# Three pairs of a second MLP product taken by quarters, seven products for eight, in the last passage of a transformer block

## The chip, the core and the metric

The kernel runs on one core of a Trainium2 chip. Five engines work side by side, each through its own list of instructions in order: TensorE (PE) multiplies, VectorE (DVE), ScalarE (ACT) and GpSimd (POOL) work on tiles of 128 partitions, and SyncE (SP) issues most of the transfers. They wait for one another through semaphores. The metric is the device time of one execution in microseconds (us).

## What is computed

```
x = A_x                                            # 2048 rows of 512, float32
h = x + attention(layernorm(x) @ wqkv) @ wo        # 32 heads, window of 8 at distance 2
r = relu(layernorm(h) @ w1 + b1)                   # 512 -> 1792
out = h + (r * r) @ w2 + b2                        # 1792 -> 512
```

## The kernel before

All matrices are split in a high and a low part of a shorter float format, and a product is the sum of three: high by high, high by low, low by high. `hi` (L152, on ScalarE) makes the high part, `lo` (L155, on VectorE or GpSimd) the low one. The 2048 rows are worked in four passages (`u` = 0 to 3) of four tiles of 128 rows. The 1792 columns of `w1` are 14 blocks `f` of 128.

In passages 0 to 2 the first product of a block is 12 matmuls of 512 columns (L231) and the second product 12 more (`mlp2`, L924), into four accumulators in PSUM, one for each row tile. These passages also hold the attention and are the same in both kernels, in instructions and in order.

The change lies in the last passage (`u` = 3), L1212 to L1271. There the blocks go in seven pairs (`PAIRS`). The **first** product of a pair is already taken by quarters with seven products for eight (Strassen's scheme in Winograd's form): `products_a` has four of the seven (24 matmuls of 256 columns, L837) and `products_b` three (18). For it the weights `w1` are loaded raw (`t_load`), combined (`t_sums`, four subtractions of 256 columns a pair, on GpSimd from the third pair) and split (`t_split`). The results are put together by additions on VectorE (L855, L867, L868, L870: each reads PSUM) and one on GpSimd (L869, `r<-u,p`), then biased, rectified and squared on ScalarE (L866, L873, L879, L884) and split (`squared`). The **second** product, `mlp2`, still takes 12 matmuls of 512 columns a block, 24 a pair. One such block follows `products_a` and one `products_b` of a later pair, and the last ones close the kernel, one row tile after the other; each finished tile is added to `h` (L932, L949) and stored. The rows `h` were given the second bias (`add_b2`, L694, on GpSimd) and put away in DRAM (`spill`) in passage 2, and come back by `unspill` in this one.

The order within an engine is written out by hand: `at(k, f, ...)` puts a call `k` slots ahead, `end_slot` runs the calls of a slot, and an engine's list is the order in which the calls are made. A `row` tile is one of 15 buffers in turn; who asks for one waits until its last user is done.

## Time and profile before

| | |
|---|---|
| median of 3 runs (lowest to highest) | 500.95 us (500.95 to 501.98) |
| the profiled execution | 500.91 us, of which the span from the first to the last instruction is 499.1 us |
| granted TensorE clock | 1.000 |
| PE busy | 494.2 us, 99% of the span, 2411 matmuls |
| PE weight load busy | 420.6 us, 84% |
| DVE, ACT, POOL busy | 383.7 (77%), 305.7 (61%), 354.6 us (71%) |
| chain that ended last | PE 98%, DMA 1% |

To read it: the chain of waits is followed back from the last instruction, at each step to what released it. Here it is TensorE nearly throughout, so that engine waits for nothing and what the others do is hidden. The shares are means over the whole kernel; the change touches the last 75 us alone, where TensorE is busy throughout and the other engines have idle stretches.

### The profile page before, as it was taken

How to read it: one execution, taken by the hardware profiler on the slowest of the kernel's cores; microseconds unless marked ns; L12 is line 12 of the kernel's file. 1: busy time of each engine (PE TensorE's matmuls, PEld its weight loads, DVE VectorE, ACT ScalarE, POOL GpSimd, SP SyncE). 2: the span in 40 equal slices, each digit the busy share in tenths (PEclk: the TensorE clock that was granted, in tenths of full speed). 3: DMA queues.
4: the chain of work that ended last, by engine and by line, in shares of the span. 5: the costliest groups of instructions: out<-in, count | busy, mean ns of one | idle time of the engine just before them, and what ended most of it. 6: DMA issues, size and time to landing. Idle time of an engine off the chain costs nothing.

```text
span 499.1 us, 7514 instructions
## 1 busy us (share of the span) xinstructions
PE 494.2 (99%) x2411; PEld 420.6 (84%) x2411; DVE 383.7 (77%) x526; ACT 305.7 (61%) x543; POOL 354.6 (71%) x429
## 2 busy tenths in 40 slices
PE   8999999999999999999999999999999999999997
PEld 7998888888888888888888888888888888998986
DVE  6479899999989989998979989897984257733233
ACT  4634778668346757478564556866454968766551
POOL 5714798996775999888878777787889353885610
PEclk9999999999999999999999999999999999999999
DMA  8779979889788899689776945977680575355212
GB/s 269 201 215 244 281 253 297 272 268 310 209 219 260 294 286 259 185 226 248 219 253 210 218 143 164 269 236 258 201 202 14 130 193 163 117 158 169 64 42 87
DMA packets 113584, 103.67 MB, mean 208 GB/s; under 512 B 33672, under 2 KB 82056, under 8 KB 113544
## 3 DMA queue, kind: packets, MB, share of 16 engines
q1 hardware_dynamic: 112600, 102.66, 70.1%
q10 hardware_dynamic: 944, 0.52, 0.3%
q8 instruction: 19, 0.31, 0.3%
q14 instruction: 21, 0.17, 0.1%
HBM read 72.65 MB, written 24.25 MB: 194 GB/s over the span
## 4 chain that ended last, share of the span: by engine, by line
PE 98%; DMA 1%; ACT 0%; ACTq 0%; DVE 0%; issue 0%
PE mm L231 49%; PE acc L924 30%; PE wo L231 9%; PE mm L837 7%; PE tr L204 2%; DMA wraw<-in_A_wqkv_dram 1%; PE half L947 0%; ACTq L570 0%; ACT big_h L152 0%; ACT xh L152 0%; DVE h L949 0%
## 5 line engine op out<-in xcount | busy, mean ns | idle before, releaser
L414 POOL TENSOR_TENSOR pr<-pr 128x512 f32<-128x512 f32 (+1 forms) x128 | 134.1, 1048 | 35.6 <-DVE pr L357 30.2
L231 PE MATMUL mm<-big_l,w_h 128*128 128x512 f32 x336 | 88.5, 390 | 0.0
L357 DVE TENSOR_TENSOR pr<-ex,v 128x1024 f32<-128x1024 f32 x62 | 75.6, 1221 | 12.0 <-POOL o L414 9.2
L344 DVE TENSOR_TENSOR pr<-qp,k 128x1024 f32<-128x1024 f32 x64 | 76.8, 1200 | 6.1 <-ACT qp L271 3.3
L380 DVE TENSOR_REDUCE ex<-pr 128x64 f32<-128x1024 f32 x64 | 78.4, 1225 | 1.8
L231 PEld LDWEIGHTS mm<-big_l,w_h 128*128 128x128 f32 x336 | 63.0, 188 | 13.4 <-ACT r L894 0.3
L155 POOL TENSOR_TENSOR rl<-r,rh 128x512 fp32r<-128x512 f32 x42 | 54.9, 1306 | 24.2 <-ACT rh L152 20.1
L231 PE MATMUL mm<-big_l,xh 128*128 128x512 f32 (+1 forms) x208 | 56.3, 379 | 0.0
L231 PE MATMUL mm<-big_h,xh 128*128 128x512 f32 (+1 forms) x208 | 53.1, 377 | 0.3 <-ACT xh L152 0.3
L231 PE MATMUL mm<-big_h,xl 128*128 128x512 f32 (+1 forms) x208 | 52.6, 374 | 0.0
L924 PE MATMUL acc<-big_h,rh 128*128 128x512 f32 x190 | 52.1, 391 | 0.0
L924 PE MATMUL acc<-big_l,rh 128*128 128x512 f32 x190 | 52.0, 390 | 0.0
L924 PE MATMUL acc<-big_h,rl 128*128 128x512 f32 x190 | 51.7, 390 | 0.0
L231 PE MATMUL mm<-big_l,w_l 128*128 128x512 f32 x168 | 44.9, 389 | 0.0
L231 PEld LDWEIGHTS mm<-big_h,xl 128*128 128x128 f32 x208 | 38.3, 188 | 6.0
L231 PEld LDWEIGHTS mm<-big_h,xh 128*128 128x128 f32 x208 | 37.9, 188 | 6.1 <-ACT xh L152 0.5
L924 PEld LDWEIGHTS acc<-big_h,rl 128*128 128x128 f32 x190 | 35.7, 188 | 7.4
L924 PEld LDWEIGHTS acc<-big_l,rh 128*128 128x128 f32 x190 | 35.6, 188 | 7.4
L231 PEld LDWEIGHTS mm<-big_l,xh 128*128 128x128 f32 x208 | 37.4, 188 | 4.9
L924 PEld LDWEIGHTS acc<-big_h,rh 128*128 128x128 f32 x190 | 35.1, 188 | 7.1 <-DVE h L932 0.3
L894 ACT ACTIVATE r<-mm,b_sb 128x512 f32<-128x512 f32 x42 | 28.7, 684 | 16.2 <-PE mm L231 15.7
L231 PEld LDWEIGHTS mm<-big_l,w_l 128*128 128x128 f32 x168 | 31.5, 188 | 6.6
(167 smaller groups left out, 919.4 us busy)
## 6 DMA issues: line engine op xcount, KB each, us to landing
k<-qkv_d SPq DMA_DIRECT2D x50, 288.0 KB, 3.2
v<-qkv_d SPq DMA_DIRECT2D x46, 288.0 KB, 3.2
qkv_d<-y SPq DMA_DIRECT2D x18, 512.0 KB, 4.0
big_l<-w2l_d SPq DMA_DIRECT2D x24, 256.0 KB, 3.1
xt<-in_A_x_dram SPq DMA_DIRECT2D x16, 256.0 KB, 4.2
q<-qkv_d SPq DMA_DIRECT2D x32, 128.0 KB, 3.6
h<-in_A_x_dram SPq DMA_DIRECT2D x16, 256.0 KB, 3.3
h_d<-h SPq DMA_DIRECT2D x16, 256.0 KB, 3.4
```

The lines of the kernel that those rows point to most:

```text
L155: eng.tensor_tensor(out=dst, in0=src, in1=h, op=ALU.subtract)
L204: nc.tensor.transpose(tr[:, k, :], src[:, k * P:(k + 1) * P], ident)
L231: nc.tensor.matmul(ps, l(k), r(k), start=(n == 0), stop=(n == 3 * KB - 1))
L344: nc.vector.tensor_tensor(out=pr.rearrange("p i w h d -> p i w (h d)"), in0=qps["now"][:, j % 2].unsqueeze(2).to_broadcast([P, RI, W, GC]) ...
L357: nc.vector.tensor_tensor(out=p2, in1=vwin, op=ALU.mult, in0=e1[:, :, :, j * GH:(j + 1) * GH].unsqueeze(4).to_broadcast([P, RI, W, GH, DH]))
L380: nc.vector.tensor_reduce(out=lf[:, :, :, j * GH:(j + 1) * GH], in_=pr, axis=X, op=ALU.add)
L414: nc.gpsimd.tensor_tensor(out=dst, in0=p2[:, :, :w], in1=p2[:, :, w:2 * w], op=ALU.add)
L837: nc.tensor.matmul(ps, sta[y][:, k], mov[x][:, k], start=(first and q == 0), stop=(last and q == len(terms) - 1), skip_group_check=True)
L894: nc.scalar.activation(r, ps, AF.Relu, bias=b1_sb[:, f:f + 1])
L924: nc.tensor.matmul(acc[j], l[:, j * P:(j + 1) * P], w[f], start=(first and n < len(js)), stop=(last and n >= len(terms) - len(js)))
```

## The change

The second products of the first four pairs stay as they are. Those of the last three pairs, (0, 7), (1, 8) and (4, 11), are taken by quarters, with seven products of 256 columns: 42 matmuls a pair in place of 24 of 512. `part` makes one of the seven. For this:

- the two blocks of `w2` of each of these pairs are loaded raw again (`v_load`, six transfers of 256 KB), combined on GpSimd (`v_sums`, four subtractions of 256 columns a pair) and split (`v_split`: two `hi` on ScalarE, two `lo` of 512 columns on GpSimd);
- the squared activations of each of these pairs, kept whole, are combined on VectorE (`s_sums`, four operations of 256 columns on two tiles in SBUF) and split (`s_split`, two `hi` on ScalarE, two `lo` on VectorE). The parts lie in columns of `w1_h` and `w1_l` that are no longer needed, as do now all split activations of this passage (`parted`), half of the first block's alone;
- seven products are summed over the three pairs in PSUM (`outer`, `inner`) and put together at the end: one copy on ScalarE, four additions of 512 columns on VectorE, and eight additions of 256 columns into `h` (two on VectorE, six on GpSimd);
- of the whole second products one now follows `products_a` of each pair, none `products_b`, and two are left after the last pair;
- the preparation of `w1` for the first products is moved ahead by one to two pairs, its raw tiles go to other buffers, and `th` is made in two halves;
- tiles 14 and 15 get the second bias after they have come back, by GpSimd, between the two last `v_split`;
- `last_tile` goes, and the last tile is finished in two halves as before, by other products.

```diff
@@ -50,6 +50,10 @@
 HL = (13, 0), (13, 1), (15, 0), (15, 1)
 ENDS = [2, 9, 3, 10]
 PAIRS = (2, 9), (3, 10), (5, 12), (6, 13), (0, 7), (1, 8), (4, 11)
+WN = 3
+PLAN = {n: (1, 0) for n in range(1, 7)}
+VS = {2: 0, 3: 1, 4: 2}
+VP = ()
...
@@ -707,6 +711,8 @@
             lambda k: wo_h[:, k, :], lambda k: wo_l[:, k, :], lows_last=t in OV)
         for n, (fn, a) in zip(slots, ((h_add, (t, ps)), (h_norm, (t,)), (add_b2, (t,)),
                                       (spill, (t,)))):
+            if fn is add_b2 and t >= 14:
+                continue
             (at if fn is h_add or fn is h_norm and t >= 14
...
     def t_split(n):
-        h, l = t_tile(n, "th", F32R), t_tile(n, "tl", F32R)
-        hi(h, tw[n])
-        for k, eng in ((2, nc.vector if n < 3 else nc.gpsimd), (0, nc.gpsimd)):
-            lo(eng, l[:, k:k + 2], tw[n][:, k:k + 2], h[:, k:k + 2])
+        h, l = t_tile("th", "pr"), t_tile("tl", "o")
+        raw = tw[n]
+        for k in (1, 0):
+            hi(h[:, 2 * k:2 * k + 2], raw[k])
+        for k, eng in ((1, nc.vector), (0, nc.gpsimd)):
+            lo(eng, l[:, 2 * k:2 * k + 2], raw[k], h[:, 2 * k:2 * k + 2])
         tw[n] = h, l
...
     def squared(f, r):
-        rh, rl = work.tile([P, D], F32R, name="rh", bufs=LAG + 1), row("rl", dt=F32R)
         nc.scalar.activation(r, r, AF.Square)
-        hi(rh, r)
-        lo(nc.vector, rl, r, rh)
-        hid[R - 1, f] = rh, rl
+        if f in PAIRS[-1]:
+            at(0, parted, f, r)
+        else:
+            parted(f, r)
+    def parted(f, r):
+        rh, rl = [w[:, :, f * P:(f + 1) * P] for w in (w1_h, w1_l)]
+        n = RI if f in WINO[:WN] else R
+        src = r.rearrange("p (j c) -> p j c", j=R)[:, :n]
+        hi(rh[:, :n], src)
+        lo(nc.vector, rl[:, :n], src, rh[:, :n])
+        hid[R - 1, f] = [lambda j, a=a: a[:, j] for a in (rh, rl)]
...
+    PLAIN = len(PAIRS) - WN
+    WINO = [p[i] for i in range(2) for p in PAIRS[PLAIN:]]
+    whole, vw = {}, {}
+    def v_load(q):
+        vw[q] = row("vraw"), row("vraw")
+        for r, f in zip(vw[q], PAIRS[PLAIN + q]):
+            nc.sync.dma_start(r, w2[f * P:(f + 1) * P, :])
+    def v_sums(q):
+        (b11, b12), (b21, b22) = [(r[:, :HD], r[:, HD:]) for r in vw[q]]
+        tt, sub = (nc.vector if q in VP else nc.gpsimd).tensor_tensor, ALU.subtract
+        tt(out=b11, in0=b12, in1=b11, op=sub)
+        tt(out=b12, in0=b22, in1=b12, op=sub)
+        tt(out=b22, in0=b22, in1=b11, op=sub)
+        tt(out=b21, in0=b21, in1=b22, op=sub)
+    def v_split(q):
+        if q == 0:
+            t = [work.tile([P, D], F32R, name="rh", bufs=LAG + 1) for _ in range(4)]
+        else:
+            t = [a[:, i] for a in [att.tile([P, 2, D], F32R, name="vs", tag=tag, bufs=3)
+                                   for tag in ("pr", "o")] for i in range(2)]
+        raw = vw[q]
+        vw[q] = t[:2], t[2:]
+        for i in range(2):
+            hi(t[i], raw[i])
+            at(int(q < 2), lo, nc.gpsimd, t[2 + i], raw[i], t[i])
+    def s_sums(n):
+        rf, rg = whole.pop(n)
+        (a11, a21), (a12, a22) = [(r[:, :HD], r[:, HD:]) for r in (rf, rg)]
+        x = whole[n] = row("x"), row("x")
+        tt, sub = nc.vector.tensor_tensor, ALU.subtract
+        tt(out=x[0][:, :HD], in0=a21, in1=a22, op=ALU.add)
+        tt(out=x[1][:, :HD], in0=a11, in1=a21, op=sub)
+        tt(out=x[0][:, HD:], in0=x[0][:, :HD], in1=a11, op=sub)
+        tt(out=x[1][:, HD:], in0=a12, in1=x[0][:, HD:], op=sub)
+    def s_split(n):
+        for x, f in zip(whole.pop(n), PAIRS[n - PLAIN]):
+            src = x.rearrange("p (j c) -> p j c", j=R)
+            h, l = [w[:, :, f * P:(f + 1) * P] for w in (w1_h, w1_l)]
+            hi(h, src)
+            lo(nc.vector, l, src, h)
+    def part(n, m, ps, js, first=False, last=False):
+        q, (f, g) = n - PLAIN, PAIRS[n]
+        c, d = PAIRS[q]
+        col, i0 = {1: (f, 0), 2: (g, 0), 4: (g, 2), 5: (c, 0), 6: (c, 2), 7: (d, 0), 3: (d, 2)}[m]
+        sta = [w[:, :, col * P:(col + 1) * P] for w in (w1_h, w1_l)]
+        lo_, hi_ = slice(0, HD), slice(HD, D)
+        if m < 4:
+            w, cs = f if m == 1 else g, hi_ if m == 3 else lo_
+            mov = w2_h[w][:, cs], w2_l[w][:, cs]
+        else:
+            i, cs = {5: (0, lo_), 7: (0, hi_), 4: (1, lo_), 6: (1, hi_)}[m]
+            mov = [t[i][:, cs] for t in vw[q]]
+        terms = [(x, y, j) for x, y in ((0, 0), (1, 0), (0, 1)) for j in js]
+        for k, (x, y, j) in enumerate(terms):
+            nc.tensor.matmul(ps[j], sta[x][:, i0 + j], mov[y], start=first and k == 0,
+                             stop=last and k >= len(terms) - len(js), skip_group_check=True)
...
-    fs = [f for pair_ in PAIRS for f in pair_]
-    need = [f for f in fs if f < 12 and f not in place]
+    fs = [f for pair_ in PAIRS[:PLAIN] for f in pair_]
+    need = [f for f in fs + WINO if f < 12 and f not in place]
...
+    AHEAD = {"0a": ((t_split, 1),), "0b": ((t_load, 3), (t_sums, 2)),
+             "1a": ((t_split, 2), (t_sums, 3)), "1b": ((t_load, 4), (t_split, 3), (t_sums, 4)),
+             "2b": ((t_load, 5), (t_split, 4), (t_sums, 5)),
+             "3b": ((t_load, 6), (t_split, 5), (t_sums, 6)), "4b": ((v_sums, 0), (t_split, 6), (v_sums, 1)), "5b": ((v_sums, 2),)}
...
     for n in range(len(PAIRS)):
-        if n + 2 < len(PAIRS):
-            t_load(n + 2)
+        if n in VS:
+            v_load(VS[n])
         products_a(n)
         if not n:
-            at(0, t_split, 1)
+            ahead("0a")
             lo(nc.vector, a_l[4], s32[4], a_h[4])
         if n:
+            if n == len(PAIRS) - 1:
+                at(0, s_sums, n - 2)
             at(0, second, n - 1)
-            if n + 1 < len(PAIRS):
-                at(0, t_split, n + 1)
-            second_product()
-        if n in (4, 5):
-            for i in range(2):
-                at(0, unspill, R * u + 2 * (n - 4) + i)
+            ahead(f"{n}a")
+            if n - 3 in VS and not VS[n - 3]:
+                at(0, v_split, 0)
+            if n == len(PAIRS) - 1:
+                at(0, s_split, n - 2)
+                at(0, v_split, 1)
+            for _ in range(PLAN[n][0]):
+                second_product()
         end_slot(5.6)
         products_b(n)
-        if n + 2 < len(PAIRS):
-            at(0, t_sums, n + 2)
-        if n > 1:
+        ahead(f"{n}b")
+        for _ in range(PLAN[n][1] if n else 0):
             second_product()
         if n == len(PAIRS) - 1:
             at(0, second, n)
-            second_product(True)
+            at(0, s_sums, n - 1)
+            at(0, s_sums, n)
+            at(0, s_split, n - 1)
+            at(0, at, 0, s_split, n)
+            for i in (2, 3, 0, 1):
+                at(1, unspill, R * u + i)
+            for i in (2, 3):
+                at(1, add_b2, R * u + i)
+            at(1, v_split, 2)
+            while used[0] < len(fs):
+                second_product()
         end_slot(4.9)
-    h = hs[S // P - 1]
-    for j in js[:-1]:
-        for f in fs[-2:]:
-            mlp2(u, f, acc, [j], False, f == fs[-1])
-            if j == 0:
-                end_slot(0.65)
-        at(0, finish, R * u + j, acc[j])
-        if j == 1:
-            at(0, nc.vector.tensor_tensor, h, acc[-1], h, ALU.add)
-        if j:
-            run(due)
-    last_tile(S // P - 1, fs[-2:])
...
+    two = {m: psum.tile([P, D], F32, name="part", tag=tag) for m, tag in zip((1, 5, 6, 7), XB)}
+    halves = {m: [t[:, j * HD:(j + 1) * HD] for j in range(RI)] for m, t in two.items()}
+    both, left, right = range(RI), slice(0, HD), slice(HD, D)
+    head, end = PLAIN, len(PAIRS) - 1
+    def outer(n):
+        for m in (1, 6, 5, 7) if n < end else (1, 6, 7, 5):
+            part(n, m, halves[m], both, n == head, n == end)
+        refill(PAIRS[n][0])
+        run(due)
+        now["slot"] += 1
+    def inner(n, m):
+        part(n, m, [acc[RI + j][:, left] for j in both], both, False, n == end)
+    for n in range(head, end):
+        outer(n)
+    inner(head, 4)
+    outer(end)
+    tt = nc.vector.tensor_tensor
+    v, u2, u3, s12, s22 = [row("c") for _ in range(5)]
+    nc.scalar.copy(v, two[1])
+    tt(out=u2, in0=two[6], in1=v, op=ALU.add)
+    tt(out=u3, in0=two[7], in1=u2, op=ALU.add)
+    tt(out=s22, in0=two[5], in1=u3, op=ALU.add)
+    tt(out=s12, in0=two[5], in1=u2, op=ALU.add)
+    for eng, i, cs, src in ((nc.gpsimd, 0, left, v), (nc.gpsimd, 1, left, v),
+                            (nc.gpsimd, 2, left, u3), (nc.gpsimd, 3, left, u3),
+                            (nc.vector, 2, right, s22), (nc.vector, 3, right, s22),
+                            (nc.gpsimd, 0, right, s12), (nc.gpsimd, 1, right, s12)):
+        h = hs[R * u + i][:, cs]
+        eng.tensor_tensor(out=h, in0=h, in1=src[:, i % RI * HD:(i % RI + 1) * HD], op=ALU.add)
+    for n in range(head + 1, end + 1):
+        inner(n, 4)
+    for i in (2, 3):
+        finish(R * u + i, acc[i])
+    z = psum.tile([P, D], F32, name="part", tag=XB[0])[:, left]
+    for m, j, ps in ((3, 0, acc[0][:, right]), (2, 0, acc[0][:, left]),
+                     (3, 1, acc[1][:, right]), (2, 1, z)):
+        for n in range(head, end + 1):
+            part(n, m, [ps, ps], [j], ps is z and n == head, n == end)
+        if m == 2 and not j:
+            finish(R * u, acc[0])
+    h = hs.pop(R * u + 1)
+    b, e = divmod(u, 2)
+    tt(out=h, in0=acc[1], in1=h, op=ALU.add)
+    nc.scalar.dma_start(out_v[b, e, 1, :, right], h[:, right])
+    tt(out=h[:, left], in0=z, in1=h[:, left], op=ALU.add)
+    nc.sync.dma_start(out_v[b, e, 1, :, left], h[:, left])
```

What stands at two places in the engines' lists, before and in the changed kernel (operation, tile written, tiles read, shape; L-numbers are each kernel's own).

GpSimd before, from the addition `r<-u,p` of the fifth pair to its last arithmetic (`traw` and `tl` are combined `w1` and its low part):

```order
L869 TENSOR_TENSOR r<-u,p 128x256
L805 TENSOR_TENSOR traw<-traw 128x2x128
L806 TENSOR_TENSOR traw<-traw 128x2x128
L807 TENSOR_TENSOR traw<-traw 128x2x128
L808 TENSOR_TENSOR traw<-traw 128x2x128
L155 TENSOR_TENSOR tl<-traw,th 128x512 x2
L869 TENSOR_TENSOR r<-u,p 128x256 x2
```

GpSimd now, from the addition `r<-u,p` of the sixth pair (`vraw` is raw `w2` being combined, `rh` and `vs` take its parts):

```order
L879 TENSOR_TENSOR r<-u,p 128x256
L159 TENSOR_TENSOR rh<-vraw,rh 128x512 x2
L924 TENSOR_TENSOR vraw<-vraw 128x256
L925 TENSOR_TENSOR vraw<-vraw 128x256
L926 TENSOR_TENSOR vraw<-vraw 128x256
L927 TENSOR_TENSOR vraw<-vraw 128x256
L879 TENSOR_TENSOR r<-u,p 128x256
L159 TENSOR_TENSOR vs<-vraw,vs 128x512 x2
L698 TENSOR_TENSOR h<-h,b_sb 128x512 x2
L159 TENSOR_TENSOR vs<-vraw,vs 128x512 x2
L1382 TENSOR_TENSOR h<-h,c 128x256 x6
```

Between the additions of the fifth and the sixth pair GpSimd now has four operations on `vraw`, one `tl` and four more on `vraw`; before the seventh pair's addition and behind it stand six low parts of `w2`, four more combinings and the two second biases, where before nothing stood.

VectorE before, from the seventh pair's `products_a` on:

```order
L855 TENSOR_TENSOR u<-mm,p 128x256
L155 TENSOR_TENSOR rl<-r,rh 128x512
L867 TENSOR_TENSOR u<-mm,p 128x256
L868 TENSOR_TENSOR r<-u,mm 128x256
L870 TENSOR_TENSOR r<-mm,u 128x256
L155 TENSOR_TENSOR rl<-r,rh 128x512 x2
L932 TENSOR_TENSOR h<-acc,h 128x512 x2
```

VectorE now, from the seventh pair's `products_b` on (`x` is a pair's combined squares, `w_l` takes low parts of activations):

```order
L877 TENSOR_TENSOR u<-mm,p 128x256
L878 TENSOR_TENSOR r<-u,mm 128x256
L880 TENSOR_TENSOR r<-mm,u 128x256
L946 TENSOR_TENSOR x<-r 128x256
L947 TENSOR_TENSOR x<-r 128x256
L948 TENSOR_TENSOR x<-x,r 128x256
L949 TENSOR_TENSOR x<-r,x 128x256
L946 TENSOR_TENSOR x<-r 128x256
L947 TENSOR_TENSOR x<-r 128x256
L948 TENSOR_TENSOR x<-x,r 128x256
L949 TENSOR_TENSOR x<-r,x 128x256
L159 TENSOR_TENSOR w_l<-x,w_h 128x4x128 x2
```

Eight operations on `x`, of the sixth and the seventh pair, now stand between the seventh pair's additions and the next low parts. Ahead of the first row, behind the seventh pair's `u<-mm,p` of `products_a`, stand four more on `x` (of the fifth pair) and three low parts of 512 columns.

## Rows read from the trace of the kernel before

**Rows 1.** The chain that ended last, from the page: by engine, by line.

```profile
PE 98%; DMA 1%; ACT 0%; ACTq 0%; DVE 0%; issue 0%
PE mm L231 49%; PE acc L924 30%; PE wo L231 9%; PE mm L837 7%; PE tr L204 2%; DMA wraw<-in_A_wqkv_dram 1%; PE half L947 0%; ACTq L570 0%; ACT big_h L152 0%; ACT xh L152 0%; DVE h L949 0%
```

**Rows 2.** The chain through the last passage: start us, us, what.

```profile
424.92 5.04 PE mm L837 x42
429.96 2.97 PE acc L924 x12
432.93 5.03 PE mm L837 x42
437.96 2.75 PE acc L924 x12
...
482.79 2.15 PE mm L837 x18
484.94 9.55 PE acc L924 x42
494.49 1.44 PE half L947 x12
...
495.96 0.42 DVE h L949
```

**Rows 3.** Engines in stretches: us, then busy (count) by engine, PEclk, DMA, GB/s.

```profile
459.00:469.50 10.50, 10.50 (x68) 9.52 (x67) 3.25 (x6) 5.80 (x11) 6.47 (x7) 1.00 0.37 121
480.10:499.10 19.00, 15.82 (x84) 13.50 (x82) 6.78 (x12) 5.62 (x10) 0.74 (x1) 1.00 0.20 71
```

**Rows 4.** GpSimd in order of time, fifth pair: start, us, operation, [idle before].

```profile
464.16 0.73 POOL L869 TENSOR_TENSOR r<-u,p 128x256 f32<-128x256 f32 x1
464.85 0.74 POOL L805 TENSOR_TENSOR traw<-traw 128x256 f32<-128x256 f32 x1
465.67 0.74 POOL L806 TENSOR_TENSOR traw<-traw 128x256 f32<-128x256 f32 x1
466.48 1.07 POOL L807 TENSOR_TENSOR traw<-traw 128x256 f32<-128x256 f32 x1
467.63 0.74 POOL L808 TENSOR_TENSOR traw<-traw 128x256 f32<-128x256 f32 x1
472.19 2.53 POOL L155 TENSOR_TENSOR tl<-traw,th 128x512 fp32r<-128x512 f32 x2 [3.82 <-ACT th L152]
```

**Rows 5.** VectorE in order of time, the same pair and the last one.

```profile
466.00 0.95 DVE L155 TENSOR_TENSOR rl<-r,rh 128x512 fp32r<-128x512 f32 x1 [1.56 <-ACT rh L152]
471.24 0.69 DVE L155 TENSOR_TENSOR rl<-r,rh 128x512 fp32r<-128x512 f32 x1 [2.63 <-ACT rh L152]
478.71 0.42 DVE L855 TENSOR_TENSOR u<-mm,p 128x256 f32<-128x256 f32 x1 [1.50 <-PE mm L837]
484.26 0.42 DVE L867 TENSOR_TENSOR u<-mm,p 128x256 f32<-128x256 f32 x1 [1.80 <-PE mm L837]
484.72 0.42 DVE L868 TENSOR_TENSOR r<-u,mm 128x256 f32<-128x256 f32 x1
```

**Rows 6.** VectorE in passage 0: two pairs of low parts, 256 columns each.

```profile
244.68 1.85 DVE L155 TENSOR_TENSOR big_l<-hnp,big_l 128x256 fp32r<-128x256 f32 x2
246.63 0.76 DVE L155 TENSOR_TENSOR big_l<-tr,big_l 128x256 fp32r<-128x256 f32 x2
```

**Rows 7.** GpSimd in order of time beside rows 6.

```profile
243.47 4.22 POOL L694 TENSOR_TENSOR h<-h,b_sb 128x512 f32<-128x512 f32 x3
```

**Rows 8.** Groups of ScalarE's instructions in the last passage: count | busy us, mean ns.

```profile
L884 ACT ACTIVATE r<-r 128x512 f32<-128x512 f32 x14 | 8.9, 633 | 0.4
L152 ACT CAST rh<-r 128x512 fp32r<-128x512 f32 x14 | 8.7, 621 | 0.4
L879 ACT ACTIVATE r<-r,b_sb 128x512 f32<-128x512 f32 x7 | 5.1, 726 | 0.0
L873 ACT ACTIVATE r<-r,b_sb 128x256 f32<-128x256 f32 x7 | 3.6, 509 | 7.3 <-DVE r L868 7.3
```

More of the change, by code (lines that the diff above doesn't have):

```diff
@@ L789, in block_kernel, with t_tile @@
     tw = {}
-    def t_tile(n, name, dt=F32):
-        return att.tile([P, KB, 2, P], dt, name=name, tag=("pr", "o")[n % 2], bufs=3)
+    def t_tile(name, tag, dt=F32R):
+        return att.tile([P, KB, 2, P], dt, name=name, tag=tag, bufs=3)
     def t_load(n):
         f = PAIRS[n][0]
-        tw[n] = t_tile(n, "traw")
+        tw[n] = [att.tile([P, RI, 2, P], F32, name="traw", tag="kv"[n % 2]) for _ in range(2)]
         for k in range(KB):
-            nc.sync.dma_start(tw[n][:, k], bass.AP(
+            nc.sync.dma_start(tw[n][k // 2][:, k % 2], bass.AP(
                 tensor=w1.tensor, offset=w1.offset + k * P * F + f * P,
@@ L802, in t_sums @@
     def t_sums(n):
-        b11, b12, b21, b22 = [tw[n][:, 2 * k:2 * k + 2, c] for k in (0, 1) for c in (0, 1)]
+        b11, b12, b21, b22 = [t[:, :, c] for t in tw[n] for c in (0, 1)]
         tt, sub = (nc.vector if n < 2 else nc.gpsimd).tensor_tensor, ALU.subtract
@@ L865, in products_b @@
         tt = nc.vector.tensor_tensor
+        if n >= PLAIN:
+            whole[n] = rf, rg
         nc.scalar.activation(rf[:, :HD], b[1], AF.Relu, bias=b1_sb[:, f:f + 1])
@@ L896, in hidden @@
         hi(rh, r)
-        at(wait, lo, nc.vector if u == R - 1 else nc.gpsimd, rl, r, rh)
-        hid[u, f] = rh, rl
+        at(wait, lo, nc.gpsimd, rl, r, rh)
+        hid[u, f] = [lambda j, a=a: a[:, j * P:(j + 1) * P] for a in (rh, rl)]
     def hidden_now():
@@ L923, in mlp2 @@
                 mid()
-            nc.tensor.matmul(acc[j], l[:, j * P:(j + 1) * P], w[f],
+            nc.tensor.matmul(acc[j], l(j), w[f],
                              start=(first and n < len(js)),
@@ L934, in finish @@
         nc.sync.dma_start(out_v[b, e, i], h)
-    def last_tile(t, fs):
-        u, i = divmod(t, R)
-        b, e = divmod(u, 2)
-        h = hs.pop(t)
-        js = slice(i * P, (i + 1) * P)
-        for c, eng in ((slice(0, D // 2), nc.sync), (slice(D // 2, D), nc.scalar)):
-            ps = turn["tr"].tile("half")[:, :D // 2]
-            terms = [(f, l, w) for f in fs for l, w in ((0, w2_h), (1, w2_h), (0, w2_l))]
-            for n, (f, l, w) in enumerate(terms):
-                nc.tensor.matmul(ps, hid[u, f][l][:, js], w[f][:, c], start=(n == 0),
-                                 stop=(n == len(terms) - 1))
-            nc.vector.tensor_tensor(out=h[:, c], in0=ps, in1=h[:, c], op=ALU.add)
-            eng.dma_start(out_v[b, e, i, :, c], h[:, c])
     def flush():
@@ L1170, in block_kernel @@
                              (13, at, 0, t_sums, 1), (13, at, 1, t_split, 0),
+                             (15, at, 0, t_load, 2),
                              (14, at, 0, turn_join, ("h", 15))):
@@ L1219, in block_kernel, with refill @@
     used = [0]
[L1221 to L1229 removed]
+    def refill(f):
         if f < 12 and need:
@@ L1232, in second_product, with ahead @@
             at(1, fetch, need.pop(0))
+    def second_product():
+        q = used[0]
+        mlp2(u, fs[q], acc, js, q == 0, q == len(fs) - 1)
+        used[0] += 1
+        refill(fs[q])
+    AHEAD = {"0a": ((t_split, 1),), "0b": ((t_load, 3), (t_sums, 2)),
+             "1a": ((t_split, 2), (t_sums, 3)), "1b": ((t_load, 4), (t_split, 3), (t_sums, 4)),
+             "2b": ((t_load, 5), (t_split, 4), (t_sums, 5)),
+             "3b": ((t_load, 6), (t_split, 5), (t_sums, 6)), "4b": ((v_sums, 0), (t_split, 6), (v_sums, 1)), "5b": ((v_sums, 2),)}
+    def ahead(step):
+        for fn, m in AHEAD.get(step, ()):
+            if fn is t_load:
+                fn(m)
+            else:
+                at(0, fn, m)
     for n in range(len(PAIRS)):
-        if n + 2 < len(PAIRS):
-            t_load(n + 2)
+        if n in VS:
+            v_load(VS[n])
         products_a(n)
         if not n:
-            at(0, t_split, 1)
+            ahead("0a")
             lo(nc.vector, a_l[4], s32[4], a_h[4])
         if n:
+            if n == len(PAIRS) - 1:
+                at(0, s_sums, n - 2)
             at(0, second, n - 1)
-            if n + 1 < len(PAIRS):
-                at(0, t_split, n + 1)
-            second_product()
-        if n in (4, 5):
-            for i in range(2):
-                at(0, unspill, R * u + 2 * (n - 4) + i)
+            ahead(f"{n}a")
[6 more added lines that the diff above has]
+                second_product()
         end_slot(5.6)
         products_b(n)
-        if n + 2 < len(PAIRS):
-            at(0, t_sums, n + 2)
-        if n > 1:
+        ahead(f"{n}b")
+        for _ in range(PLAN[n][1] if n else 0):
             second_product()
```

9 lines of the change are left out of this document (removed).

## The prediction

> **What bounds the kernel now.** I read the chain that ended last first [rows 1]: TensorE has 98% of it, so what counts is how long TensorE's list is and whether it ever waits. Then the same chain through the last passage, the only one in which the order of work differs [rows 2]: pieces of first product (L837) and second product (L924) follow each other without a piece of another engine between them until the last addition. The reader should see there the price of each piece: 24 matmuls of 256 columns with 12 of 512 behind them, and so on. The granted clock is 1.00 throughout [rows 3], the higher of the two levels, 2.4 GHz. The other engines have room before the change: in the 10.5 us of one pair DVE is busy 3.25 us, ACT 5.80 and POOL 6.47, and in the last 19 us POOL has 0.74 us of work [rows 3]. The question is whether they still keep ahead when TensorE's pair gets shorter and they get more to do.
>
> **TensorE's own sum.** A block of 512 columns costs 2.75 us for 12 matmuls, 0.229 each; of 256 columns 18 cost 2.15 us, 0.1194 each [rows 2]. Before, the second product takes one piece of 2.97 (0.22 of it a wait that stays), nine more of 2.75, then 9.55 and 1.44: 38.49 us without that wait. After: four pairs of 24 (96 x 0.229 = 22.00) and three of 42 (126 x 0.1194 = 15.04), 37.04 us. That is 1.45 us less, half a microsecond a pair, and all that the change can gain. The tail behind the last matmul is of the same kind (one addition of 256 columns, 0.42 us [rows 2], and a transfer of 128 KB), so I put it at nothing either way; two halves that queue behind three whole tiles could cost some tenths.
>
> The Trainium skill ("TensorE: Matmul & The Clock Gate", Back-to-back issue gap) gives N/2.4 + 2.5 ns for one matmul after another, which would be 215.8 and 109.2 ns here. By it a pair would save 24 x 0.2158 - 42 x 0.1092 = 0.59 us, three pairs 1.78, and the forecast would be 0.3 us lower. The rows are longer than the formula at both sizes, and the sum goes by the rows.
>
> **TensorE's new timetable, if nothing waits.** The piece of 12 that ends at 432.93 is the first in both kernels [rows 2]. From there a pair is 5.03 + 2.75 = 7.78 us, where before 2.75 more followed. Five of them end at 471.83, the last `products_b` (2.15) at 473.98, two whole second products at 479.48. Each `outer` is 24 x 0.1194 = 2.87 us: fifth pair to 482.35, sixth to 485.22; the inner product 0.72, to 485.94; seventh pair to 488.81; then 48 matmuls, to 494.54, against 495.94 now. That is the 1.40 again. Two deadlines follow. The sixth pair's second part needs the low half of its combined activations after eight matmuls, at 482.35 + 0.96 = **483.3**. The seventh pair's needs the second low part of its `w2` after ten, at 485.94 + 1.19 = 487.1.
>
> **GpSimd against VectorE.** What the rows show: two low parts of 256 columns on VectorE, read from SBUF, took 1.85 us together while GpSimd worked through three biases, and two of the same size that read PSUM took 0.76 beside the third of these [rows 6, 7]. A low part of 512 columns took 0.95 beside GpSimd and 0.69 without; the GpSimd operation next to the first took 1.07 in place of 0.74 [rows 4, 5]. So an operation with both inputs in SBUF and one of GpSimd go one after the other, and where both have a queue they take turns. 1.85 less two of 0.38 leaves 1.09 us for the one turn that VectorE waited. A turn behind a 512-column operation of GpSimd (1.27 us each, 2.53 for two [rows 4]) thus makes a VectorE operation of 256 columns last about 1.43 in place of 0.38; behind a 256-column one (0.74) I take about 0.95.
>
> The Trainium skill ("SBUF — State Buffer", Who interferes with whom) says the same as a rule: a VectorE instruction with two SBUF inputs and a GpSimd instruction that reads SBUF exclude each other for the whole instruction. The rule speaks against this change, since all twelve `s_sums` operations and all eight new low parts on VectorE are of that kind. By it every turn costs a whole instruction, as I take it; without it the forecast would be the first rival below.
>
> Now GpSimd's list. The fifth pair's `products_b` ends at 456.27 + 2.15 = 458.4, so its `r<-u,p` starts no earlier than then. Behind it stand four combinings (start to start 0.82 [rows 4], 3.28), `tl` 1.27, four more 3.28, the sixth pair's `r<-u,p` 0.70, two low parts 2.53, four combinings 3.28: with the first 0.70, 15.0 us. The seventh pair's `r<-u,p` is reached at 473.4 without one wait, and its input is there at 473.98 - 0.1. Nothing is spare. The VectorE operations with two SBUF inputs in that stretch (four low parts, four on `x`, three more low parts) must fit between: 4 to 5 us of it, some in the 0.1 to 0.2 us gaps between dependent combinings. I put it at 477, bounds 474.5 and 478.5.
>
> VectorE's list is the other side. After the seventh pair's first `u` (ready about 1.7 us after `products_a` starts [rows 2, 5], 468) come four on `x` and three low parts. Alone they are 4 x 0.38 + 3 x 0.61 = 3.4 us, done before the `u` of `products_b` at 473.3. Taking turns with two low parts of 512 and four combinings on GpSimd they are 3.4 + 2 x 1.1 + 4 x 0.5 = 7.6, and they start at about 469, behind GpSimd's late sixth `r<-u,p`: to 476.5. The three additions (0.46 apart [rows 5]) end at 477.9. GpSimd is then in its `r<-u,p`, two low parts and two biases, all but the first of 512 columns. The sixth pair's four `x` operations wait one turn each: about 1 us for the first, then 4 x 1.4, to 483.5. The seventh pair's four meet an empty GpSimd, 1.6, to 485.1; then the low half that the 483.3 deadline wants, 0.69: **485.8. TensorE waits 2.5 us** there. Bounds: without any turn the `x` of the sixth pair end at 476.2, the seventh pair's wait for ScalarE's chain (0.51 + 0.63 + 0.73 + 0.63 [rows 8] from 473.8: 476.3) and end at 478, the low half at 478.8, so 4.5 us are spare and TensorE waits 0; with two more turns it waits 4.
>
> The next deadline moves with it to 489.6. ScalarE makes six high parts (at most 0.62 each [rows 8], one of half the size) after the `x` at 483.5, the last two those of `w2`, to 487.0; GpSimd's two low parts take turns with VectorE's, 1.27 + 0.4 each, to 490.3. **0.7 us more.** Bounds 0 and 1.5. Unspilled rows that arrive late would lengthen this one, for the biases stand ahead of these two low parts in GpSimd's list, and SP's loads wait for `row` buffers that the same VectorE queue frees.
>
> **Moves that cost nothing.** The loads of raw `w1` and `w2` are issued a pair or more ahead, with the DMA engines 0.37 busy in a pair [rows 3]; half as long a `th` in two pieces is the same work; the split activations in `w1`'s columns take fewer buffers, and half of one is left out. The biases of tiles 14 and 15 leave a place where GpSimd hid them, and in the new place they are the two turns counted above. Shorter pairs leave 7.78 us for about 6 us of ScalarE, 5 of GpSimd and 3.5 of VectorE in the first four pairs; if a turn falls badly there, a few tenths of a wait (0 to 0.5, I take 0.1).
>
> **Sum.** 495.94 - 1.40 + 2.5 + 0.7 + 0.1 = 497.8 at the last matmul, 1.9 later than now. The profiled execution took 500.91 us for a span of 499.1, and stands 0.04 below the median of 500.95: 500.9 + 1.9 = 502.8 us.
>
> **The rivals.**
> *Faster: the turns do not line up.* If GpSimd's seventh `r<-u,p` comes by 474.5 and the four `x` of the sixth pair fall between its low parts, the low half is ready before 483.3 and all of the 1.4 remains: 499.5 us. Against it: GpSimd's list is full without a single turn. For it: the spare 4.5 us, and 8% less of GpSimd's time would do. It decides when TensorE's waits are under 0.4 us.
> *No difference: half of the turns.* Waits of 0.4 to 2.4 us together, at the same two places: 499.9 to 501.9.
> *Slower still: the rows of `h` come late* and hold GpSimd's biases and what stands behind them, the last low parts and the six additions into `h`; each microsecond past 490.3 is TensorE's. With 1.5 more, 504.3. Here also belongs a fall of the granted clock after the waits: the rest of 11 us at the 1.2 GHz level would cost several us, but no row shows a wait of TensorE of this length before, so I can only bound it.
> *The seven products do not cost less.* The 256-column row excludes this: 42 x 0.1194 is below 24 x 0.229 by 0.48.
>
> **How the numbers follow.** Forecast (waits over 2.4 us, 501.9 to 503.9) 0.49, slower still 0.08, no difference 0.23, faster 0.20. A measurement of this kernel tells about 0.2% (1 us) from no change: faster 0.20, same 0.23, slower 0.57. The range leaves out the end of the faster case and the slower one's: 499.7 to 503.9. The forecast's own range is 501.9 to 503.9.
>
> **What would show it.** In the profile after: pieces of 7.78 us a pair to 474; one wait of TensorE's weight loads or matmuls at the sixth pair's second part, released by VectorE's `w_l`, and a shorter one released by GpSimd's `vs`; the four `x` operations about 1.4 us apart and the GpSimd operations beside them lengthened. If they are 0.4 apart and TensorE does not wait, the turns were wrong. If TensorE waits inside the first four pairs, the timetable is wrong. If the last matmul to the end is much over 3.2 us, the tail is.

## The result, and the profile after

| | before | after |
|---|---|---|
| median (lowest to highest) of 6 runs each | 501.06 us (500.95 to 501.98) | 503.45 us (502.77 to 504.00) |
| ratio after / before, 95% interval | | 1.0043 (1.0031 to 1.0056) |
| the profiled execution, and its span | 500.91 us, 499.1 us | 502.77 us, 500.6 us |
| PE busy, matmuls | 494.2 us, 2411 | 493.5 us, 2459 |
| DVE, ACT, POOL busy | 383.7, 305.7, 354.6 us | 403.7, 312.5, 373.1 us |

The changed kernel is 2.4 us slower, 0.43%. The prediction was 502.8 us, slower, with 499.7 to 503.9 as its range. The six runs of after fall into two groups, 502.77 to 503.08 and 503.82 to 504.00 us, and none lies at the median; the profiled one is the lowest.

The page of after: the span; the busy time, share and instructions of each engine; then the chain that ended last, its shares by engine and by line.

```profile
span 500.6 us, 7710 instructions
...
PE 493.5 (99%) x2459; PEld 422.9 (84%) x2459; DVE 403.7 (81%) x553; ACT 312.5 (62%) x563; POOL 373.1 (75%) x449
...
DVE 3%; PE 2%; issue 0%
DVE w_l L159 1%; PE acc L972 1%; PE part L972 1%; DVE x L946 0%; DVE x L948 0%; DVE x L947 0%; DVE x L949 0%; DVE h L1398 0%; DVE r L880 0%; DVE u L877 0%; DVE r L878 0%
```

TensorE is busy 0.7 us less, and yet the kernel is longer. The chain [rows 1] had 98% on TensorE. The shares after are of the short piece that the page follows, about the last 25 us, and VectorE has more of it than TensorE: what ends last now goes through its combined activations (`x`, L946 to L949) and low parts (`w_l`, L159). The same chain in order of time (start us, us, what):

```profile
475.46 0.60 DVE w_l L159
...
477.24 0.33 DVE x L946
477.57 1.44 DVE x L947
479.01 1.45 DVE x L948
...
481.80 1.52 DVE x L946
483.32 0.34 DVE x L947
...
484.45 4.95 DVE w_l L159 x5
...
489.45 2.17 PE part L972 x16
491.62 4.68 PE acc L972 x39
496.30 1.09 PE part L972 x9
...
497.42 0.42 DVE h L1398
```

From 475.46 to 489.45 us no piece of TensorE is on it. The last addition starts at 497.42, before at 495.96 [rows 2]: 1.46 later. TensorE in order of time at the two places where it stands still (the bracket is the idle time before a row, and what ended it):

```profile
482.66 0.40 PE L972 MATMUL part<-vs,w_h 128*128 128x256 f32 x2
485.11 0.50 PE L972 MATMUL part<-vs,w_l 128*128 128x256 f32 x2 [2.05 <-DVE w_l L159]
485.44 0.64 PE L972 MATMUL part<-vs,w_h 128*128 128x256 f32 x4
...
488.56 0.40 PE L972 MATMUL part<-vs,w_h 128*128 128x256 f32 x2
489.45 0.50 PE L972 MATMUL part<-vs,w_l 128*128 128x256 f32 x2 [0.48 <-DVE w_l L159]
489.79 0.64 PE L972 MATMUL part<-vs,w_h 128*128 128x256 f32 x4
```

From 482.66 to 485.44 it starts four matmuls, which take 0.48 us elsewhere: 2.30 us lost. From 488.56 to 489.79 it loses 0.75 in the same way. Elsewhere in the passage it loses 0.22 us, in the products of the third pair (see below). GpSimd beside it:

```profile
476.54 0.74 POOL L879 TENSOR_TENSOR r<-u,p 128x256 f32<-128x256 f32 x1 [1.63 <-DVE u L877]
477.24 2.93 POOL L159 TENSOR_TENSOR vs<-vraw,vs 128x512 fp32r<-128x512 f32 x2
480.12 2.91 POOL L698 TENSOR_TENSOR h<-h,b_sb 128x512 f32<-128x512 f32 x2
485.76 3.08 POOL L159 TENSOR_TENSOR vs<-vraw,vs 128x512 fp32r<-128x512 f32 x2 [2.73 <-ACT vs L156]
```

Four GpSimd operations of 512 columns lie between 477.24 and 483.03. In that stretch of the chain stand four long `x` operations, three of the sixth pair and the first of the seventh (the chain shows the third of them, L949, in two pieces, left out here); when GpSimd has nothing to do (483.0 to 485.8) the next one takes 0.34 of the chain.

### The profile page after: what moved, and what is told of

It is laid out like the page before. It is cut to its first block, busy times and chain, and to the rows that moved or that the text cites. A ratio compares the mean times of both kernels' runs of the same rounds, so it can differ in the third digit from the quotient of the medians.

```text
span 500.6 us, 7710 instructions
## 1 busy us (share of the span) xinstructions
PE 493.5 (99%) x2459; PEld 422.9 (84%) x2459; DVE 403.7 (81%) x553; ACT 312.5 (62%) x563; POOL 373.1 (75%) x449
## 5 line engine op out<-in xcount | busy, mean ns | idle before, releaser
L159 POOL TENSOR_TENSOR rl<-r,rh 128x512 fp32r<-128x512 f32 x42 | 54.9, 1308 | 24.4 <-ACT rh L156 20.0
L1008 PE MATMUL acc<-big_l,rh 128*128 128x512 f32 x144 | 38.7, 390 | 0.0
L1008 PE MATMUL acc<-big_h,rl 128*128 128x512 f32 x144 | 38.5, 389 | 0.0
L1008 PE MATMUL acc<-big_h,rh 128*128 128x512 f32 x144 | 38.5, 389 | 0.0
L540 ACT COPY y<-mm 128x512 f32<-128x512 f32 x36 | 21.1, 586 | 25.5 <-PE mm L235 24.4
L418 POOL TENSOR_TENSOR o<-pr 128x128 f32<-128x128 f32 x64 | 31.0, 484 | 5.0
L1008 PEld LDWEIGHTS acc<-big_h,rl 128*128 128x128 f32 x144 | 27.0, 188 | 5.6
```

The costliest lines, as they stand in the source:

```text
L159: eng.tensor_tensor(out=dst, in0=src, in1=h, op=ALU.subtract)
L418: nc.gpsimd.tensor_tensor(out=dst, in0=p2[:, :, :w], in1=p2[:, :, w:2 * w], op=ALU.add)
L540: nc.scalar.copy(dst, src)
L1008: nc.tensor.matmul(acc[j], l(j), w[f], start=(first and n < len(js)), stop=(last and n >= len(terms) - len(js)))
```

## The experiments

Two theories went into the first four. **Turns**: a VectorE operation with both inputs in SBUF and a GpSimd operation exclude each other, and where both have a queue VectorE waits one whole GpSimd operation for each of its own; that makes the low halves late. **Lists**: the pair has become shorter, and VectorE's and ScalarE's lists are too long for it, whatever GpSimd does. The edits of e1 to e3, e5 and e7 are against the changed kernel, that of e4 against the kernel before; e6 is e5 with the lines shown.

**e1: the biases back in their old place**

(In the kernel before the biases of tiles 14 and 15 run in the first pairs of the last passage, at 432.48 and 435.90 us, and not in passage 2 as the description of that kernel has it.)

```diff
-            if fn is add_b2 and t >= 14:
-                continue
...
-            for i in (2, 3):
-                at(1, add_b2, R * u + i)
             at(1, v_split, 2)
```

> The changed kernel with one part undone: the second bias of tiles 14 and 15 is added where the kernel before adds it, in the first pairs of the last passage; the seven products stay. In the changed kernel TensorE loses 2.2 us in front of the sixth pair's second part and 0.65 us in the seventh pair's. Theory of the turns: of the four x operations of VectorE that last 1.4 to 1.5 us in place of 0.41, two stand beside the two biases; without them 2 x 1.1 = 2.2 us come back, the first wait is 0 to 0.5 us, the second stays 0.4 to 0.9; 502.8 - 2.2 = 500.6 us, plus up to 1.5 us if GpSimd's list in the first pairs, 2.5 us longer by the two biases, now holds TensorE there: 500.6 to 502.1. Rival, the lists of VectorE and ScalarE are too long for the shorter pair, whatever GpSimd does: the x operations still end at 485 and TensorE still waits 2.2 us: 502.8 or more.

Measured: 504.09 us (503.91 to 504.45), ratio 1.0064 (1.0049 to 1.0079). TensorE's waits, and GpSimd in the third pair (start, us, operation, idle before):

```profile
444.81 0.50 PE L843 MATMUL mm<-big_l,w_h 128*128 128x256 f32 x2 [0.99 <-ACT r L874]
...
487.07 0.50 PE L970 MATMUL part<-vs,w_l 128*128 128x256 f32 x2 [0.42 <-DVE w_l L159]
...
439.87 1.29 POOL L698 TENSOR_TENSOR h<-h,b_sb 128x512 f32<-128x512 f32 x1
441.12 1.19 POOL L877 TENSOR_TENSOR r<-u,p 128x256 f32<-128x256 f32 x1
```

The time is a miss, the wait is not (504.09 lies where the lists put it, but by the lists the wait of 2.2 stays). The wait in front of the sixth pair's second part goes from 2.05 to 0.42, as the turns say. But the second bias now stands at 439.87 ahead of `r<-u,p`, which runs 2 us later than in the changed kernel, counted from the start of the passage; ScalarE's chain and TensorE's next products wait for it. From the third pair's `products_b` to the fifth's `products_a` TensorE falls 2.6 us back (by the starts of its pieces in both kernels), where I had allowed 1.5. The profiled execution had also begun the passage 1.0 us late. So the new place of the biases is a trade: with seven products GpSimd has no room for them in the first pairs either.

**e2: the biases behind the last low parts**

```diff
-            for i in (2, 3):
-                at(1, add_b2, R * u + i)
             at(1, v_split, 2)
+            for i in (2, 3):
+                at(1, at, 0, add_b2, R * u + i)
```

> The changed kernel with the two biases of tiles 14 and 15 still added on reload, but behind the seventh pair's two last low parts in GpSimd's list instead of ahead of them; nothing else differs. Theory of the turns: GpSimd is then idle beside the last x operations of the sixth pair and the first of the seventh, two of the four long ones go from 1.5 to 0.41 us, the first wait shrinks from 2.2 to 0 to 0.5 us; the second stays 0.3 to 0.9; the six additions into h come some 2 us later, with 4 us to spare until the last matmul: 500.3 to 501.0 us, below the changed kernel and at or just under the kernel before. Rival, the lists are too long by themselves: no change, 502.8. Rival, late rows of h are what costs: the last low parts start earlier and the second wait goes, the first stays: 502.1.

Measured: 501.64 us (501.40 to 501.93), ratio 1.0009 (1.0000 to 1.0019). VectorE's `x` at the end of the sixth pair and the start of the seventh, the only row of TensorE in the passage with idle time before it, and a wait of VectorE's last additions:

```profile
479.47 1.51 DVE L948 TENSOR_TENSOR x<-x,r 128x256 f32<-128x256 f32 x1
481.01 0.43 DVE L949 TENSOR_TENSOR x<-r,x 128x256 f32<-128x256 f32 x1
481.36 0.42 DVE L946 TENSOR_TENSOR x<-r 128x256 f32<-128x256 f32 x1
...
487.94 0.74 PE L972 MATMUL part<-vs,w_h 128*128 128x256 f32 x4 [0.29 <-POOL vs L159]
...
493.34 2.10 DVE L1016 TENSOR_TENSOR h<-acc,h 128x512 f32<-128x512 f32 x3 [0.63 <-POOL h L1382]
```

Two of the four long operations fell from 1.4 and 1.5 us to 0.43 and 0.42, and of the first wait 0.23 us is left, too little for a row of its own. The same instructions in another order on GpSimd are worth 1.8 us. That rules out the lists: VectorE, ScalarE and TensorE have the same work in the same order here. Late rows of `h` are ruled out too, since with them the first wait would have stayed. The time is still 0.6 over the expected 500.3 to 501.0. The profile shows 0.5 of it: VectorE's additions wait 0.63 for GpSimd's, and the last one starts 0.53 behind the end of the last matmul (496.24 for 495.71), in place of 0.04.

**e3: GpSimd's pieces in halves**

```diff
-            at(int(q < 2), lo, nc.gpsimd, t[2 + i], raw[i], t[i])
+            for cs in (slice(0, HD), slice(HD, D)):
+                at(int(q < 2), lo, nc.gpsimd, t[2 + i][:, cs], raw[i][:, cs], t[i][:, cs])
```

(and the two late biases likewise)

> The changed kernel with the same work in the same order, but GpSimd's low parts of w2 and the two late biases written as two instructions of 256 columns each in place of one of 512. This changes one size: what one turn of GpSimd costs. Theory of the turns (VectorE waits for one whole GpSimd instruction and then has its go): beside these pieces the x operations take 0.9 to 1.0 us in place of 1.4 to 1.5, but there are twice as many pieces to meet, so more of the x operations are lengthened; the first wait falls from 2.2 to 0.8 to 1.8 us, the second stays or grows by some tenths: 501.5 to 503.0 us. Rival, the two engines share a bandwidth and a VectorE operation is slowed by the same factor as long as GpSimd is busy: the x operations still take 1.4 to 1.5 us beside GpSimd; 502.8 or more, for GpSimd's list gets longer by eight starts of an instruction.

Measured: 502.56 us (502.20 to 502.89), ratio 1.0032 (1.0020 to 1.0043). VectorE's second `x` of the sixth pair and first of the seventh, and GpSimd beside them:

```profile
477.43 0.96 DVE L949 TENSOR_TENSOR x<-r 128x256 f32<-128x256 f32 x1
...
480.08 0.96 DVE L948 TENSOR_TENSOR x<-r 128x256 f32<-128x256 f32 x1
...
477.18 3.57 POOL L159 TENSOR_TENSOR vs<-vraw,vs 128x256 fp32r<-128x256 f32 x4
```

0.96 in place of 1.5, for the same elements on GpSimd in the same order: what VectorE waits is one instruction of the other, not a share of a bandwidth. Seven of the eight `x` operations of the two pairs are now lengthened, by 0.4 to 0.55, in place of four by 1.0 to 1.1, so the lengthening falls only from 4.3 to 3.7 us in all. TensorE's first wait is 1.35, and the time 0.8 to 0.9 us better.

**e4: the biases late in the kernel before**

```diff
+            if fn is add_b2 and t >= 14:
+                continue
...
+            for i in (2, 3):
+                at(0, add_b2, R * u + i)
```

> The kernel before with only the other part of the change: the second bias of tiles 14 and 15 is added behind the last pair's GpSimd work, on the reloaded rows, and the second product stays whole. Theory of the turns: GpSimd has 0.74 us of work in the last 19 us there and VectorE no queue of operations with two SBUF inputs, so two GpSimd operations of 1.3 us meet nothing that TensorE waits for: 500.6 to 501.1 us, no difference (the first pairs lose 2.5 us of GpSimd's work, which nobody waits for). Rival, late rows of h or biases on reload cost by themselves: 501.5 or more.

Measured: 501.19 us (500.67 to 502.64), ratio 1.0007 (0.9998 to 1.0017): no difference. Biases on reload cost nothing by themselves; they cost where VectorE has a queue of the kind that they lock out.

**e5: two pairs instead of three**

```diff
-WN = 3
+WN = 2
-VS = {2: 0, 3: 1, 4: 2}
+VS = {3: 0, 4: 1}
```

(`s_sums`, `s_split`, `v_sums` and `v_split` of the fifth pair go)

> Seven products for the last two pairs instead of three (four whole second products then stand ahead of the first outer part in place of two); the biases stay where the changed kernel has them. TensorE's list is 0.4 us longer than in the changed kernel, 0.8 shorter than before. Theory of the turns: VectorE has four x operations and three low parts less, GpSimd four combinings and two low parts less, and the sixth pair's deadline stays; the x operations beside GpSimd's low parts are still 1.5 us long, but they end at 482, ahead of it: TensorE's waits of 2.2 and 0.65 us both go. Then the end is no longer TensorE's: behind the last outer part VectorE has nine operations (four c at 0.70, two h, three additions from PSUM at 0.7) of some 7 us and TensorE only 3.6 us of work, so the last addition ends some 2 us behind the last matmul: 501.8 to 502.8 us. Rival, waits come from the seven products' own dependencies and not from the two engines' queues: TensorE waits about 1.4 to 2.9 us for two pairs as well. Rival, the tail fits beside: 500.3 to 500.9 us.

Measured: 502.02 us (501.89 to 502.89), ratio 1.0021 (1.0012 to 1.0030). The last of the long `x`, TensorE's last matmul, and VectorE's last additions:

```profile
478.96 1.52 DVE L946 TENSOR_TENSOR x<-r 128x256 f32<-128x256 f32 x1
...
494.52 0.28 PE L972 MATMUL part<-big_l,w_h 128*128 128x256 f32 x1
...
494.03 1.87 DVE L1016 TENSOR_TENSOR h<-acc,h 128x512 f32<-128x512 f32 x3
495.82 0.68 DVE L1391 TENSOR_TENSOR h<-acc,h 128x512 f32<-128x512 f32 x1
496.60 0.42 DVE L1393 TENSOR_TENSOR h<-part,h 128x256 f32<-128x256 f32 x1
```

As the turns expected: four long `x` again, but done in time, and no row of TensorE in the passage has idle time before it. Its last matmul starts 1.1 us earlier than before (495.64). The end is VectorE's, 1.8 us behind the last matmul. With TensorE's waits gone a new bound stood behind them, as said.

**e6: as e5, one whole second product behind the last outer part**

```diff
-            while used[0] < len(fs):
+            while used[0] < len(fs) - 1:
                 second_product()
...
     outer(end)
+    second_product()
```

> As e5_two_pairs, but one of the four whole second products (2.75 us of TensorE) goes behind the last outer part, so that VectorE's nine last operations lie beside TensorE's work. Theory of the turns: the sixth pair's deadline is 2.75 us earlier than in e5, at about 482.9, and the low half is ready at 482 to 482.5: waits 0 to 0.5 us in all; the last addition follows the last matmul by 0.3 to 0.5 us, at 495.1 to 495.6 against 496.0 before and 497.4 in the changed kernel: 500.2 to 501.0 us, under both. Rival, a seven-product form does not get under the kernel before because it pays its 0.8 us back in waits wherever they lie: 501.0 to 502.

Measured: 500.75 us (500.40 to 501.38), ratio to before 0.9992 (0.9983 to 1.0001), and 2.6 us under the changed kernel (503.35) on the same chip. The last matmul and the last two additions:

```profile
495.24 0.28 PE L972 MATMUL part<-big_l,w_h 128*128 128x256 f32 x1
...
494.90 0.69 DVE L1392 TENSOR_TENSOR h<-acc,h 128x512 f32<-128x512 f32 x1
495.70 0.42 DVE L1394 TENSOR_TENSOR h<-part,h 128x256 f32<-128x256 f32 x1
```

No row of TensorE in the passage has idle time before it; at the seventh pair's low half, near 487 us, it loses 0.3, within the 0 to 0.5 expected. The last addition starts 0.46 behind the start of the last matmul. It is the best of the versions, but 0.08% under the kernel before is not to be told from none: the 0.8 us of two pairs is about what a start of the program varies by (in this profile TensorE stood idle for 0.81 us at 5.1 us).

**e7: three pairs, biases behind, low parts in halves**

(the two edits of e2 and e3, the biases in one piece each)

> Three pairs, the biases behind the last low parts as in e2_bias_behind, and GpSimd's low parts of w2 in two instructions of 256 columns each as in e3_halves (the biases whole). In e2 TensorE still waited 0.44 us for the second of GpSimd's last two low parts, and the last addition came 0.5 us late behind GpSimd's additions into h. Theory of the turns: VectorE's last four low parts pay 0.5 instead of 1.1 us a turn, GpSimd's pieces get their go sooner, and the wait shrinks to 0 to 0.2 us; the additions into h start 0.2 to 0.5 us sooner: 500.8 to 501.4 us against 501.64 in e2. Rival, the starts of twice as many instructions eat it: 501.6 or more.

Measured: 501.30 us (500.90 to 501.80), ratio 1.0005 (0.9996 to 1.0014), 0.3 under e2, as expected in size, though the two intervals overlap. One step of it was wrong:

```profile
487.39 0.74 PE L973 MATMUL part<-vs,w_h 128*128 128x256 f32 x4 [0.44 <-POOL vs L159]
```

The wait for GpSimd's last low part did not shrink (0.29 in e2). In the profile the gain is at the two other places: the 0.23 left of the first wait is gone, and VectorE's last additions no longer wait for GpSimd's.

**e8 to e11: the changed kernel again**

> The changed kernel itself, unaltered, for the spread: its six runs fell into two groups, spans of 500.6 to 500.9 and of 501.7 to 501.9 us. Theory that the longer group waits longer in the last passage (the rows of h, the granted clock): a profile of a long run shows waits of TensorE behind 480 us that are 1 us longer, or a granted clock under 1.00 while TensorE works. Rival, the difference is made in the first microseconds of the program, where TensorE waits for its first loads: a long run shows it before 10 us, and the last passage is the same to 0.2 us. 502.7 to 504.0 us.

Measured: 503.35 us (502.75 to 503.98), ratio 1.0045 (1.0031 to 1.0058). The profile of e8 was of a short run and shows the same waits, 2.05 and 0.48. e9 to e11 are three more executions.

> The changed kernel once more, for a profile of one of its longer runs: in ten runs the span was 500.6 to 500.9 us with a mean granted clock of 1.000 in five and 501.5 to 501.9 with 0.995 to 0.997 in five. Theory that the granted clock falls for some microseconds after TensorE's wait of 2.2 us: a long run shows a granted clock of 0.5 in a stretch behind 485 us in which TensorE works, and matmuls of 256 columns 0.24 us apart in place of 0.12 there. Rival, the clock falls only behind the last matmul and the microsecond is lost elsewhere: at the first loads before 10 us, or in a longer wait. A short run decides nothing.

> The same look again: a long run (span over 501.3 us) is what tells the theories of e9 apart; a short one (500.6 to 500.9) decides nothing.

> The same look again, with the same two theories as in e9: a granted clock of 0.5 behind 485 us while TensorE works, or a microsecond lost elsewhere with the clock at 1.00 until the last matmul.

Measured: e9 504.12, e10 503.24, e11 503.62 us. e9 is a long run with a mean granted clock of 0.997. Three stretches behind the wait that ends at 485.7 in it (us, then PE busy and matmuls, PEclk, DMA share, GB/s), and in the second block TensorE in order of time:

```profile
485.70:487.00 1.30, 1.30 (x10) 0.95 0.00 0
487.00:488.50 1.50, 1.50 (x9) 0.50 0.05 11
488.50:490.20 1.70, 1.70 (x10) 0.50 0.00 0
```

```profile
485.69 0.50 PE L972 MATMUL part<-vs,w_l 128*128 128x256 f32 x2 [2.05 <-DVE w_l L159]
...
488.33 0.63 PE L972 MATMUL acc<-rh,w_h 128*128 128x256 f32 x2
488.76 0.63 PE L972 MATMUL acc<-rh,w_l 128*128 128x256 f32 x2
```

The granted clock is 0.50, 1.2 GHz, from about 486.8 to 490.1 us while TensorE works, and two matmuls of 256 columns start 0.43 us apart in place of 0.24. The 16 matmuls of that stretch cost 1.5 us more; in return the second wait is gone, for VectorE's low part is there by then. What is left is 0.7 us (last matmul 498.43, 0.6 of it from a later start, against 497.10). In the profile of after the same stretch has 1.00 throughout. e10 and e11 have a clock of 1.00; e11's 501.5 is a start of the passage 0.8 us later and nothing else. So each of the two theories was seen in one long run. Of the 13 runs of the changed kernel six have a mean clock of 0.995 to 0.997 (median 503.99 us) and seven 1.000 (503.04). That all six are of e9's kind was seen in one of them alone. Nor does the mean show it by itself: in the profiles of e2 and e5, both 0.998, the clock falls only after 497 us, behind the last matmul.

## Why the prediction was right, and where its steps were off

The direction, the mechanism and the size came out. That the profiled execution met the forecast to 0.03 us is luck: terms that were off by some tenths cancelled, and one of them I had not seen at all.

**TensorE's timetable.** I put the end of the last `products_b` at 473.98, of the two second products at 479.48 and of the fifth pair's `outer` at 482.35. They came at 473.60, 479.07 and 481.94, all about 0.4 earlier. 0.16 of that is in the reckoning: 432.93 is where the chain has the next piece, but its first matmul starts at 432.77. The passage began 0.21 earlier (421.67 against 421.88), and the short wait in the first piece of twelve [rows 2], which I took to stay, was gone. Against that TensorE lost 0.22 in the third pair, whose 42 products took 5.25 us where those of the other pairs take 5.03:

```profile
442.75 0.40 PE L845 MATMUL mm<-big_l,w_h 128*128 128x256 f32 x2
443.04 0.51 PE L845 MATMUL mm<-big_l,th 128*128 128x256 f32 x2
443.38 0.40 PE L845 MATMUL mm<-big_l,tl 128*128 128x256 f32 x2
```

These rows start 0.29 and 0.34 apart, where 0.24 is usual, and a little more is lost 1 us later. I had allowed 0.1 us of waits in the first four pairs; the profile does not say what made this one.

**The gain.** Forecast 1.40 us, measured 1.37. The last addition starts 1.46 later. The two waits make 3.05 and the third pair 0.22; the earlier start takes off 0.21 and the short wait that was gone 0.23. That would be 2.83 later, so 1.37 is what the shorter list gave. By the formula of the Trainium skill ("TensorE: Matmul & The Clock Gate", Back-to-back issue gap) it would have been 1.78; the new rows of 256 columns start 0.120 us apart, as those of before did, not 0.109, so the rows were the better base.

**The first wait.** Forecast 2.5 us, measured 2.30, in the place and by the releaser named. The chain behind it: GpSimd's seventh `r<-u,p` at 477 (476.5); the sixth pair's `x` to 483.5 (to 481.8); the seventh's to 485.1 (484.4); the low half at 485.8 against a deadline of 483.3 (485.1 against 482.9). The price of a turn was 1.43 us for an operation of 0.38: 1.51 for 0.41. I had counted four turns for the sixth pair and none for the seventh; it was three and one. One cause was wrong: GpSimd's list was not full. It stood idle for 1.63 us before 476.54 and waited for VectorE's `u`, so the lateness was VectorE's own, from the turns of the fifth pair:

```profile
469.89 1.51 DVE L947 TENSOR_TENSOR x<-r 128x256 f32<-128x256 f32 x1
...
474.24 1.83 DVE L159 TENSOR_TENSOR w_l<-x,w_h 128x512 fp32r<-128x512 f32 x2
475.99 0.41 DVE L877 TENSOR_TENSOR u<-mm,p 128x256 f32<-128x256 f32 x1
```

The rule of the Trainium skill that I drew on ("SBUF — State Buffer", Who interferes with whom: VectorE with two SBUF inputs and GpSimd exclude each other for the whole instruction) is what e2 and e3 show: 1.51 beside 512 columns, 0.96 beside 256, 0.42 beside none.

**The second wait.** Forecast 0.7, measured 0.75, but by another releaser. It was not GpSimd's `vs` that came last but VectorE's own low part of the seventh pair, locked out in its turn by GpSimd's last two. With the biases out of the way (e1, e2, e7) GpSimd's is last, as I had it.

**The rest.** The tail behind the last matmul at nothing: right, 3.1 us of span from the start of the last addition before and 3.2 after. What I had not seen as a term at all: the time around the span is 2.17 us after, 1.81 before. It is 0.36 of the 1.86 us by which the profiled executions differ, and it made up for the last matmul, which ended at 497.38 where I had 497.8. It goes with the kernel and not with the execution: 1.75 to 1.91 us in 48 runs of the kernel before, 2.09 to 2.20 in the 13 of the changed one, 2.20 to 2.28 in the ten of e2, 1.78 to 1.91 in the eleven of e6. What makes it I can't say.

**The rivals.** The first and second (no turns, half of them) are out by the rows above. "Slower still" had two parts. Late rows of `h` did not show. The granted clock that falls behind TensorE's wait, which I could not price, did, in one of the five profiles of the changed kernel, for 0.7 us. The median is 0.65 over the forecast because three of its six runs, with a mean clock of 0.997, lie about 1 us over the other three. That the clock made them longer is likely from e9 but not shown: the passage also begins up to 0.8 us later from one profile of the changed kernel to another.

**Where the gain went.** 1.37 us off TensorE's list were paid back as 3.05 of waits. e2 takes 2.2 of these away without touching TensorE's or VectorE's list. Even then the kernel does not get under the one before.

## What to carry to other kernels

When work is moved to an engine off the critical path, ask what kind of instruction it is, not only how long it takes: twelve VectorE operations of 0.41 us with both inputs in SBUF were cheap by the sum, and cost TensorE 2.3 us because they stood behind GpSimd operations, four of them each behind one of 512 columns. The order within GpSimd's list is then worth more than its length, and smaller GpSimd instructions make a cheaper turn. Where a wait goes, look for what ends second: in e5 it was VectorE's last nine operations, and one product of TensorE's put behind the last part hid them again.

## What the runs showed of the hardware

- A turn is priced by the other engine's instruction: a VectorE operation of 256 columns took 0.42 us beside an idle GpSimd, 0.96 beside operations of 256 columns and 1.51 beside operations of 512. Operations that read PSUM were not lengthened beside GpSimd (0.42 at 476.83 in after, `r<-mm,u`, while GpSimd's `r<-u,p` ran from 476.54 to 477.28).
- After a wait of 2.05 us the granted clock fell to 1.2 GHz for 3.3 us in one profiled execution of the changed kernel and stayed at 2.4 GHz in four others with a wait of 2.05 to 2.08. Waits of 0.99 us (e1) and 1.35 (e3) were followed by none in their profiles.
- Each time that TensorE starts again after a wait in these profiles, the first two matmuls of 256 columns take 0.33 to 0.34 us in place of 0.24 (485.11 to 485.44 and 489.45 to 489.79 above).
